# Attention in quads of heads: the last keys of four heads as one unit of 64x64 quadrants, totals in two passes, wider exponentials, three weight blocks without ScalarE

## The chip, the cores and the metric

The kernel runs on one core of one Trainium2 chip. The metric is the time of one execution on the device, in microseconds (us). TensorE is called PE here, VectorE DVE, ScalarE ACT, GpSimd POOL and SyncE SP, as in the profile; PEld is PE's load of weights. Nearly all bulk transfers are issued by SP.

## The reference

Soft-capped attention over 24 heads (2 batches of 12) of 448 tokens and 64 features, followed by two feed-forward layers of 768 to 2048 to 768 features on the 896 tokens:

```python
scores = scale * np.matmul(q, k.transpose(0, 1, 3, 2))
scores = cap * np.tanh(scores / cap)
attn = np.exp(scores - np.max(scores, axis=-1, keepdims=True))
attn = attn / (np.sum(attn, axis=-1, keepdims=True) + 1e-09)
attn_out = np.matmul(attn, v)
...
h = x @ w_in          # x: attention's result, 896 x 768
g = np.where(h >= 1, h, np.where(h <= -1, 0.0, (h + 1) ** 2 / 4))
x = g @ w_out
...
h = x @ moe2_w_in
out = np.maximum(0.01 * h, h) @ moe2_w_out
```

The attention is in float32. The weights of the layers arrive as 64-bit numbers; the kernel turns each into a float32 and splits that, like the activations, into a rounded high part and a low rest, so that a product of the layers is three matmuls (high by high, low by high, high by low).

## The kernel before

**Attention.** The heads are taken in pairs `i` (12 of them). The 448 keys of a head are three full chunks of 128 and a last one of 64. `scores(i, c)` multiplies the keys of chunk `c` by all 448 queries: the two heads of the pair lie in the two halves of the 128 rows of PE's array, so that a unit is two matmuls of 64 rows by 128 columns. The last chunk is different: POOL copies the 64 last keys of both heads into a block-diagonal tile `KL` (and the values into `VL`, L310), and the unit is four matmuls of 128 rows by 32 columns, half of whose stationary operand is zero. ACT takes the tanh of a unit out of PSUM (L336, 896 elements per partition, 448 for the last chunk) and the exponential over two chunks at once in SBUF (L339, 1792 and 1344 elements). `values(i, c)` multiplies the exponentials by the values, in four matmuls of 128 by 32 per chunk, and adds up over the chunks in one of two PSUM tiles that alternate from pair to pair. `sums` adds the exponentials of the three full chunks on DVE (L354); `totals`, in `normalize`, sums them over the keys by a matmul with ones (L364), four matmuls of 128 by 32. The rest of `normalize` brings the result to SBUF (L380), collects the totals by four small transfers (L372), takes the reciprocal (L376), spreads it over the partitions by way of DRAM (L385, L387) and leaves the result as a high and a low part, `xh` and `xl` (L389 to L392).

**Order.** Nothing is ordered by hand on the five engines. Each step is a task of `Plan` with a cost and what it reads and writes; PE's tasks keep the order in which the program adds them, and `Plan.order` places all others by when they could start and by how urgent they are. The order is then fixed: each engine, and SP's queue, works it off from first to last.

**Layers.** `weights(g)` loads block `g` (768 KB for the first layer) and makes the high and low part: an absolute value on ACT (L223), a clamp, a shift and two combinations on DVE (L204 to L217), the high part by a copy on ACT (L228), the low part on DVE. The first four blocks are loaded and made while attention still runs. Then 2304 matmuls of 128 by 128 by 448 columns follow, of the lines 237, 238 and 241. The first 18 of them (`in_part(0, ...)`, batch 0) stand within the last pair, so that PE has work while the last exponentials are taken; then come the other three blocks for batch 0, then the first four feature chunks of batch 1, and last the two that hang on the results of the last heads.

Of the kernel before, what the change touches and what calls it, by code (L numbers as in the profile page):

```python
# [19 lines left out]
LOW_30 = 0x3FFFFFFF  # L20

# [103 lines left out]
def tile_softcap_attention_ffn_ffn(  # L125
# [67 lines left out]
    def weights(g, after=()):  # L193
# [29 lines left out]
        add("ACT", act(n) + 0.06, lambda: nc.scalar.activation(f32(w), f32(r[:, :, 1]), AF.Abs), R, [W])  # L223
# [4 lines left out]
        add("ACT", act(n), lambda: nc.scalar.copy(h, f32(w)), [W], [H])  # L228
# [18 lines left out]
    NIN, NE, NX = 3, 2, 4  # L247
    WARM = 7

    Q = [ap.tile([P, S], F32, name=f"q{n}") for n in range(NIN)]  # L250
    K = [ap.tile([P, S], F32, name=f"k{n}") for n in range(NIN)]
    KL = [ap.tile([P, P], F32, name=f"kl{n}") for n in range(NIN)]

    V = [ap.tile([P, NC, P], F32, name=f"v{n}") for n in range(NIN)]
    VL = [ap.tile([P, P], F32, name=f"vl{n}") for n in range(NIN)]
# [3 lines left out]
    E = [[ap.tile([P, k, S], F32, name=f"e{x}{n}") for n, k in enumerate((4, 3))] for x in range(NE)]  # L259
    T = [ap.tile([P, 2, S], F32, name=f"t{n}") for n in range(NE)]  # L260
    XS = [ap.tile([P, 2, S], F32, name=f"xs{n}") for n in range(NX)]
    zero = ap.tile([P, S], F32, name="zero")
    CS = [ap.tile([P, 2, SP7], F32, name=f"cs{n}") for n in range(NX)]
    RC = [ap.tile([P, SP7], F32, name=f"rc{n}") for n in range(NX)]
    BC = [ap.tile([P, S], F32, name=f"bc{n}") for n in range(NX)]
    XF = [ap.tile([P, S], F32, name=f"xf{n}") for n in range(NX)]
    RR = [dram.tile([2, S], F32, name=f"rr{n}") for n in range(NX)]
# [5 lines left out]
    def q_load(i, j, by):  # L273
        by.dma_start(out=Q[i % NIN][HEADS[j]], in_=qt[i][HEADS[j], j])

    def begin():
        nc.scalar.dma_start(out=K[0], in_=kt[0])
        for j in range(2):
            q_load(0, j, nc.scalar if j else nc.sync)
# [3 lines left out]
        for _ in range(WARM):  # L283
            nc.tensor.matmul(DS[3][:, 0, :S], z[:, :P], z, start=True, stop=True)
# [4 lines left out]
        for n in range(NIN):  # L289
            nc.gpsimd.memset(KL[n], 0.0)  # L290
            nc.gpsimd.memset(VL[n], 0.0)
# [7 lines left out]
    def loads(i):  # L299
        z = i % NIN  # L300
        if i:
            dma(lambda: nc.sync.dma_start(out=K[z], in_=kt[i]), P * S * 4, (), [("k", z)])
            for j in range(2):
                dma(lambda j=j: q_load(i, j, nc.sync), D * S * 4, (), [("q", z, j)])
        dma(lambda: nc.sync.dma_start(
            out=V[z].rearrange("p c x -> p (c x)"), in_=vt[i].rearrange("p c j d -> p (c j d)")), P * NC * P * 4, (), [("v", z)])

        def last(to, src, at):
            for r, x in zip(HEADS, at):
                nc.gpsimd.tensor_copy(to[r, r], src[r, x:x + LAST])  # L310

        add("POOL", 0.6, lambda: last(KL[z], K[z], (S - LAST, 0)), [("k", z)], [("kl", z)])
        add("POOL", 0.6, lambda: last(VL[z], V[z][:, L], (0, D)), [("v", z)], [("vl", z)])

    def part(i, c):

        return E[i % NE][c // 2][:, c % 2 * 2:c % 2 * 2 + (1 if c == L else 2)]

    def scores(i, c):
        z, t = i % NIN, i * NC + c  # L320
        d, e = DS[t % 2], part(i, c)
        last = c == L
        whole, key = E[i % NE][c // 2], ("e", i % NE, c // 2)

        def mm():
            if last:
                for r in COLS4:
                    nc.tensor.matmul(d[r, 0, :S], KL[z][:, r], Q[z], start=True, stop=True)  # L328
                return
            for j, r in enumerate(HEADS):  # L330
                at = c * P + (LAST if j else 0)
                nc.tensor.matmul(d[:, j, :S], K[z][r, at:at + P], Q[z][r], start=True, stop=True)  # L332

        n = 1 if last else 2
        add("PE", PE_F, mm, [("kl" if last else "k", z), ("q", z, 0), ("q", z, 1)], [("d", t % 2)])
        add("ACT", act(n * S, 1), lambda: nc.scalar.activation(e, d[:, :n, :S], AF.Tanh, scale=rcap),  # L336
            [("d", t % 2)], [key])
        if c % 2:
            add("ACT", act((2 + n) * S, 1), lambda: nc.scalar.activation(whole, whole, AF.Exp, scale=capb), [], [key])  # L339

    def values(i, c):
        z, e, a = i % NIN, part(i, c), DS[2 + i % 2]
        v = VL[z] if c == L else V[z][:, c]

        def mm():
            for n, r in enumerate(COLS4):
                nc.tensor.matmul(a[r, 0, :S], v[:, r], e[:, 0 if c == L else n // 2], start=(c == 0), stop=(c == L))  # L347

        add("PE", PE_F, mm, [("e", i % NE, c // 2), ("vl" if c == L else "v", z)], [("d", 2 + i % 2)])

    def sums(i, c):

        t = T[i % NE]
        add("DVE", vec(2 * S), lambda: nc.vector.tensor_tensor(  # L354
            out=t, in0=part(i, 0) if c == 1 else t, in1=part(i, c), op=ALU.add), [("e", i % NE, c // 2)], [("t", i % NE)])

    def normalize(i):
        a, t, e = DS[2 + i % 2], T[i % NE], part(i, L)

        def totals():  # L360

            for n, r in enumerate(COLS4):
                w, x = (ones[0], t[:, n]) if n < 2 else (ones[n - 1], e[:, 0])
                nc.tensor.matmul(a[r, 1, :S], w, x, start=True, stop=True)  # L364

        add("PE", PE_F, totals, [("e", i % NE, 1), ("t", i % NE)], [("d", 2 + i % 2)])
        y = i % NX
        xs, cs, rc, bc, xf, rr = XS[y], CS[y], RC[y], BC[y], XF[y], RR[y]

        def total(k, j):  # L370
            row = k * D + j * Q4
            nc.sync.dma_start(out=cs[HEADS[j], k], in_=xs[row:row + 1, 1])  # L372

        def recip():
            nc.vector.tensor_tensor(out=cs[:, 0], in0=cs[:, 0], in1=cs[:, 1], op=ALU.add)
            nc.vector.reciprocal(out=rc, in_=cs[:, 0])  # L376

        b, hp = divmod(i, NP)
        hi, lo = (x[:, hp, b * S:(b + 1) * S] for x in (xh, xl))
        add("DVE", vec(2 * S), lambda: nc.vector.tensor_copy(xs, a[:, :, :S]), [("d", 2 + i % 2)], [("xs", y)])  # L380
        for k in range(2):
            for j in range(2):
                dma(lambda k=k, j=j: total(k, j), 0, [("xs", y)], [("cs", y, k, j)], more=1.0)
# [9 lines left out]


    later = {}
    turn = [0]

    def bank():
        turn[0] += 1
        return (2, 0, 1, 3)[(turn[0] - 1) % 4]  # L400
# [75 lines left out]
    for i in range(NIN - 1):  # L476
        loads(i)
# [112 lines left out]
```

## Time and profile before

| what | before |
|---|---|
| median of 3 runs | 567.0 us (565.86 to 567.14) |
| the profiled execution's own time | 566.49 us |
| its span (first to last instruction) | 564.7 us |
| PE busy | 558.3 us (99%) |
| DVE busy | 396.8 us (70%) |
| ACT busy | 273.3 us (48%) |
| POOL busy | 21.4 us (4%) |
| bytes read from HBM, written | 61.74 MB, 2.80 MB |

The span is 1.8 us shorter than the execution's time. Busy shares are means over a program with two very different stages: attention until about 100 us after the start, the layers from there on. PE is busy nearly always in both, so its busy share alone can't tell how much of its time is needed; for that, the starts of its instructions have to be read, one group after the other. The records of a float32 matmul come in twos (it runs as two passes), so a unit of two matmuls shows as x4 and a unit of four as x8.

### The profile page before, as it was taken

Reading aid. Unit: us, or ns where it says so; the run is one execution under the profiler, and the core shown is the slowest. Engines: PE = TensorE matmul, PEld = TensorE weight load, DVE = VectorE, ACT = ScalarE, POOL = GpSimd, SP = SyncE. Lnnn points to the kernel's source line nnn. Section 1 sums busy time; section 2 is a strip of 40 time slices with the busy share of each in tenths; the row PEclk is TensorE's granted clock in tenths of the full one; section 3 lists DMA queues with packets and bytes.
Section 4 is the critical chain, followed back from the end, with each engine's and each line's share of the span. In section 5 each row is a group of like instructions: output and inputs, shape, how many; then the busy total and the mean of one; then the engine's idle time right before and its main releaser. Section 6 shows DMA issues by size and latency. Waiting matters only on the chain.

```text
span 564.7 us, 7882 instructions
## 1 busy us (share of the span) xinstructions
PE 558.3 (99%) x3031; PEld 463.7 (82%) x3031; DVE 396.8 (70%) x586; ACT 273.3 (48%) x332; POOL 21.4 (4%) x64
## 2 busy tenths in 40 slices
PE   8999999999999999999999999999999999999997
PEld 4332334899999999999999999999999999999996
DVE  2486979849999987756665859988877755646420
ACT  6999998047666655332332335544444432232210
POOL 4221210000000000000000000000000000000000
PEclk9999999999999999999999999999999999999999
DMA  8454653423333323443324333433323144453400
GB/s 223 142 156 139 163 142 94 142 73 112 113 113 115 106 79 95 129 113 111 110 81 156 140 111 114 156 122 113 96 79 107 38 125 132 139 142 93 136 33 34
DMA packets 27622, 65.14 MB, mean 115 GB/s; under 512 B 8384, under 2 KB 14528, under 8 KB 27584
## 3 DMA queue, kind: packets, MB, share of 16 engines
q1 hardware_dynamic: 27328, 64.29, 37.6%
q8 instruction: 24, 0.39, 0.3%
q10 hardware_dynamic: 224, 0.34, 0.2%
q14 instruction: 14, 0.11, 0.1%
q0 software_dynamic: 32, 0.00, 0.0%
HBM read 61.74 MB, written 2.80 MB: 114 GB/s over the span
## 4 chain that ended last, share of the span: by engine, by line
PE 95%; ACT 1%; DMA 1%; DVE 1%; issue 0%; SPq 0%; DVEq 0%; ACTq 0%; POOLq 0%
PE d L237 27%; PE d L241 27%; PE d L238 27%; PE d L347 6%; PE d L332 4%; PE d L364 2%; PE d L328 1%; DMA capb<-cap 1%; ACT e L336 1%; ACT e L339 1%; DMA cs<-xs 0%; DVE t L354 0%; SPq L372 0%; DVE w L212 0%; DVE w L208 0%
## 5 line engine op out<-in xcount | busy, mean ns | idle before, releaser
L237 PE MATMUL d<-gh,whi 128*128 128x448 f32 x384 | 140.3, 365 | 0.0
L238 PE MATMUL d<-gl,whi 128*128 128x448 f32 x384 | 140.2, 365 | 0.0
L237 PE MATMUL d<-xh,whi 128*128 128x448 f32 x384 | 139.5, 363 | 0.0
L238 PE MATMUL d<-xl,whi 128*128 128x448 f32 x384 | 139.2, 362 | 0.0
L228 ACT CAST whi<-w 128x512 fp32r<-128x512 f32 (+1 forms) x80 | 56.4, 705 | 137.7 <-PE d L238 89.3
L241 PE MATMUL d<-xh,wlo 128*128 128x448 f32 x384 | 111.9, 362 | 0.0
L241 PE MATMUL d<-gh,wlo 128*128 128x448 f32 x384 | 111.7, 365 | 0.0
L171 DVE TENSOR_TENSOR wlo<-w,whi 128x512 fp32r<-128x512 f32 (+1 forms) x80 | 63.4, 792 | 54.3 <-ACT whi L228 54.2
L237 PEld LDWEIGHTS d<-xh,whi 128*128 128x128 f32 x384 | 72.1, 188 | 6.5 <-DVE xs L380 0.7
L241 PEld LDWEIGHTS d<-gh,wlo 128*128 128x128 f32 x384 | 72.1, 188 | 5.7
L237 PEld LDWEIGHTS d<-gh,whi 128*128 128x128 f32 x384 | 72.1, 188 | 5.7
L238 PEld LDWEIGHTS d<-gl,whi 128*128 128x128 f32 x384 | 72.1, 188 | 5.7
L241 PEld LDWEIGHTS d<-xh,wlo 128*128 128x128 f32 x384 | 72.1, 188 | 4.7
L238 PEld LDWEIGHTS d<-xl,whi 128*128 128x128 f32 x384 | 72.1, 188 | 4.7
L223 ACT ACTIVATE w<-wr 128x512 f32<-128x512 f32 (+1 forms) x80 | 61.4, 767 | 16.2 <-DVE wlo L171 6.7
L212 DVE SCALAR_TENSOR_TENSOR w<-wr,w 128x512 int32<-128x512 int32 (+1 forms) x80 | 63.9, 798 | 2.4
L216 DVE SCALAR_TENSOR_TENSOR w<-wr,w 128x512 int32<-128x512 int32 (+1 forms) x80 | 63.8, 797 | 2.4
L429 DVE TENSOR_TENSOR a<-d,a 128x896 f32<-128x896 f32 x32 | 34.7, 1086 | 16.2 <-ACT a L428 15.8
L336 ACT ACTIVATE e<-d,rcap 128x896 f32<-128x896 f32 (+1 forms) x48 | 41.4, 909 | 7.2 <-PE d L332 3.9
L208 DVE TENSOR_SCALAR w<-w 128x512 int32<-128x512 int32 (+1 forms) x80 | 38.5, 481 | 2.7
L204 DVE TENSOR_SCALAR w<-w 128x512 f32<-128x512 f32 (+1 forms) x80 | 37.7, 472 | 3.5 <-ACT w L223 3.5
L339 ACT ACTIVATE e<-e,capb 128x1792 f32<-128x1792 f32 (+1 forms) x24 | 38.5, 1603 | 0.8
(48 smaller groups left out, 373.8 us busy)
## 6 DMA issues: line engine op xcount, KB each, us to landing
wr<-w1o SPq DMA_DIRECT2D x24, 512.0 KB, 3.6
wr<-w2i SPq DMA_DIRECT2D x16, 768.0 KB, 4.3
wr<-w2o SPq DMA_DIRECT2D x24, 512.0 KB, 3.7
wr<-w1i SPq DMA_DIRECT2D x11, 768.0 KB, 4.3
wr<-w1i SPq DMA_DIRECT2D x15, 256.0 KB, 3.2
v<-vt SPq DMA_DIRECT2D x12, 256.0 KB, 3.3
bc<-rr SPq DMA_DIRECT2D x24, 112.0 KB, 4.0
out<-a SPq DMA_DIRECT2D x12, 224.0 KB, 4.3
```

What stands on the lines that cost most here:

```text
L171: nc.vector.tensor_tensor(out=out_, in0=x, in1=f32(hi), op=ALU.subtract)
L204: nc.vector.tensor_scalar(out=f32(w), in0=f32(w), scalar1=W_MIN, scalar2=W_MAX, op0=ALU.max, op1=ALU.min)
L208: nc.vector.tensor_scalar(out=w, in0=w, scalar1=3, scalar2=LOW_30, op0=ALU.logical_shift_left, op1=ALU.bitwise_and)
L212: nc.vector.scalar_tensor_tensor(out=w, in0=r[:, :, 1], scalar=SIGN_AND_TOP, in1=w, op0=ALU.bitwise_and, op1=ALU.bitwise_or)
L216: nc.vector.scalar_tensor_tensor(out=w, in0=r[:, :, 0], scalar=29, in1=w, op0=ALU.logical_shift_right, op1=ALU.bitwise_or)
L223: add("ACT", act(n) + 0.06, lambda: nc.scalar.activation(f32(w), f32(r[:, :, 1]), AF.Abs), R, [W])
L228: add("ACT", act(n), lambda: nc.scalar.copy(h, f32(w)), [W], [H])
L237: nc.tensor.matmul(o[:, b, :S], ch, h[:, f, r], start=first, stop=False)
L238: nc.tensor.matmul(o[:, b, :S], ch, l[:, f, r], start=False, stop=False)
L241: nc.tensor.matmul(o[:, b, :S], cl, h[:, f, r], start=False, stop=last)
L336: add("ACT", act(n * S, 1), lambda: nc.scalar.activation(e, d[:, :n, :S], AF.Tanh, scale=rcap), [("d", t % 2)], [key])
L339: add("ACT", act((2 + n) * S, 1), lambda: nc.scalar.activation(whole, whole, AF.Exp, scale=capb), [], [key])
```

## The change

Attention is now done in steps `j` of two pairs, that is four heads (6 steps).

- The last keys of the four heads are one unit, `AB`: each head's 64 keys by 64 features take one quadrant of 64 by 64 of PE's array, four matmuls, without the zeros, so the tiles `KL` and `VL` and POOL's copies go. A step has seven units (A0, A1, A2 of the first pair, B0, B1, B2 of the second, and AB) for scores and seven for values, where two pairs had eight and eight.
- The results of a step are added up in one PSUM tile (bank 0 for the first pair, bank 1 for the second); the other three tiles are a ring for scores and totals. Before it was two and two.
- The totals of a step are one unit of its own in a slot of the ring, in two passes: first AB's exponentials against ones, then the sums of the full chunks.
- The exponentials are taken over groups of two, three and two units (1792, 2688 and 1792 elements). They have one, two and one buffers.
- Queries, keys and values are loaded for two pairs at a time, in two buffers instead of three of one pair; the reciprocals and the last steps of `normalize` run over two pairs at once.
- For the first three weight blocks the absolute value and the copy are done by DVE (`early`).
- At the end, the 18 matmuls of `in_part(0, ...)` stand in three pieces of 6 around the last values and totals, and the last two feature chunks of batch 1 are one piece.

```diff
-    def weights(g, after=()):
+    def weights(g, after=(), early=False):
...
+        def absolute():
+            nc.vector.tensor_scalar(out=w, in0=r[:, :, 1], scalar1=LOW_31, scalar2=None, op0=ALU.bitwise_and)
...
+        if early:
+            add("DVE", vec2(n), absolute, R, [W])
+        else:
+            add("ACT", act(n) + 0.06, lambda: nc.scalar.activation(f32(w), f32(r[:, :, 1]), AF.Abs), R, [W])
...
+        if early:
+            add("DVE", vec2(n), lambda: nc.vector.tensor_copy(h, f32(w)), [W], [H])
...
+    A0, A1, A2, B0, AB, B1, B2 = UNITS = range(7)
+    GROUPS = [(A0, A1), (A2, B0, AB), (B1, B2)]
+    CHUNK = {A0: (0, 0), A1: (0, 1), A2: (0, 2), B0: (1, 0), B1: (1, 1), B2: (1, 2)}
+    WHERE = {u: (g, n) for g, us in enumerate(GROUPS) for n, u in enumerate(us)}
+    NE = [1, 2, 1]
...
+    RING, AV = 3, 3
+    def slot():
+        ring[0] += 1
+        return (ring[0] - 1) % RING
...
+    def scores(j, u):
+        z, s = j % NIN, slot()
...
+            for h, r in enumerate(HEADS):
+                if u == AB:
+                    at = 0 if h else S - LAST
+                    for p, c in enumerate(HEADS):
+                        nc.tensor.matmul(d[c, h, :S], K[z][r, p, at:at + LAST], Q[z][r, p], start=True, stop=True)
+                    continue
+                p, c = CHUNK[u]
+                at = c * P + (LAST if h else 0)
+                nc.tensor.matmul(d[:, h, :S], K[z][r, p, at:at + P], Q[z][r, p], start=True, stop=True)
...
+    def values(j, u):
...
+                if u == AB:
+                    for p, k in enumerate(HEADS):
+                        nc.tensor.matmul(DS[AV][r, p, :S], V[z][k, p, L, r], e[k, h], start=False, stop=p == 0)
+                    continue
...
+    def results(j):
+        y = j % NX
+        for p in range(2):
+            add("DVE", vec(S), lambda p=p: nc.vector.tensor_copy(XS[y][:, p], DS[AV][:, p, :S]), [("av", p)], [("xs", y, p)])
...
+            for x in range(2):
+                for n, r in enumerate(COLS4):
+                    p, h = divmod(n, 2)
+                    w, e = (ones[0], T[j % NT2][p][:, h]) if x else (ones[1 + p], part(j, AB)[:, h])
+                    nc.tensor.matmul(DS[s][r, 0, :S], w, e, start=x == 0, stop=x == 1)
...
+    for j in range(NQ + 1):
+        now, prev = j < NQ, j > 0
+        if now:
+            units(scores, j, (A0, A1))
...
+        else:
...
+            in_part(0, first[0], [0], range(2))
+        if prev:
+            units(values, j - 1, (B1, B2))
+            results(j - 1)
+        if now:
+            units(scores, j, (A2, B0, AB))
+            sums(j, 1)
+        else:
+            in_part(0, first[0], [0], range(2, 4))
...
+        if prev:
+            normalize(j - 1)
+            if j + 1 < NQ:
+                loads(j + 1)
+        if now:
+            units(values, j, (A0, A1))
+            units(scores, j, (B1, B2))
+            sums(j, 2)
...
+            units(values, j, (A2, B0, AB))
```

The first place is PE's queue in the middle of attention. Before, one pair (`d_66`, `d_67` are the tiles for scores, `d_68`, `d_69` those for results and totals; L332 and L328 are scores, L347 values, L364 totals):

```order
L332 MATMUL d_66<-q_88,k_91 128x448 x2
L328 MATMUL d_67<-q_88,kl_94 32x448 x4
L347 MATMUL d_68<-e_105,v_97 32x448 x8
L332 MATMUL d_66<-q_89,k_92 128x448 x2
L332 MATMUL d_67<-q_89,k_92 128x448 x2
L347 MATMUL d_68<-e_106,v_97 32x448 x4
L347 MATMUL d_68<-e_106,vl_100 32x448 x4
L364 MATMUL d_68<-t_109,ones_102 32x448 x2
L364 MATMUL d_68<-e_106,ones_103 32x448
L364 MATMUL d_68<-e_106,ones_104 32x448
```

Now, from A2 to the end of a step; ahead of these rows the step has A0 and A1 and the values of the last step's B1 and B2 (L360 and L356 are scores, L381 and L377 values, L412 totals; `d_69` holds the results):

```order
L360 MATMUL d_68<-q_87,k_89 128x448 x2
L360 MATMUL d_66<-q_87,k_89 128x448 x2
L356 MATMUL d_67<-q_87,k_89 64x448 x4
L412 MATMUL d_68<-e_98,ones_94 32x448 x2
L412 MATMUL d_68<-e_98,ones_95 32x448 x2
L412 MATMUL d_68<-t_102,ones_93 32x448 x2
L412 MATMUL d_68<-t_103,ones_93 32x448 x2
L381 MATMUL d_69<-e_96,v_91 32x448 x8
L360 MATMUL d_66<-q_87,k_89 128x448 x2
L360 MATMUL d_67<-q_87,k_89 128x448 x2
L381 MATMUL d_69<-e_97,v_91 32x448 x8
L377 MATMUL d_69<-e_97,v_91 64x448 x4
```

The shape of the last keys' unit and its place changed, and the totals of the step before now stand in the middle of a step, in the slot that A2 of this step has just left.

The second place is ACT's queue in the middle of attention. Before, with the absolute value (L223) and the copy (L228) of the second weight block between tanh (L336) and exponentials (L339):

```order
L336 ACTIVATE e_105<-d_66,rcap 128x896
L336 ACTIVATE e_105<-d_67,rcap 128x896
L339 ACTIVATE e_105<-e_105,capb 128x1792
L223 ACTIVATE w_73<-wr_71 128x768
L336 ACTIVATE e_106<-d_66,rcap 128x896
L336 ACTIVATE e_106<-d_67,rcap 128x448
L339 ACTIVATE e_106<-e_106,capb 128x1344
L336 ACTIVATE e_107<-d_66,rcap 128x896
L336 ACTIVATE e_107<-d_67,rcap 128x896
L339 ACTIVATE e_107<-e_107,capb 128x1792
L228 CAST whi_76<-w_73 128x768
```

Now, one whole step (L365 is tanh, L368 the exponential):

```order
L365 ACTIVATE e_96<-d_67,rcap 128x896
L365 ACTIVATE e_96<-d_68,rcap 128x896
L368 ACTIVATE e_96<-e_96,capb 128x1792
L365 ACTIVATE e_97<-d_66,rcap 128x896
L365 ACTIVATE e_97<-d_67,rcap 128x896
L365 ACTIVATE e_97<-d_68,rcap 128x896
L368 ACTIVATE e_97<-e_97,capb 128x2688
L365 ACTIVATE e_99<-d_67,rcap 128x896
L365 ACTIVATE e_99<-d_68,rcap 128x896
L368 ACTIVATE e_99<-e_99,capb 128x1792
```

In the new queue no weight block stands between the first tanh and the last exponential of attention: blocks 0 to 2 are DVE's, and block 3 comes after the last exponential.

The third place is DVE's queue at the end of attention: how the results of the last heads (`xf_131` before, `xf_116` now) come out. Before:

```order
L204 TENSOR_SCALAR w_73<-w_73 128x768
L208 TENSOR_SCALAR w_73<-w_73 128x768
L212 SCALAR_TENSOR_TENSOR w_73<-wr_71,w_73 128x768
L389 TENSOR_TENSOR xf_130<-xs_113,bc_126 128x448
L391 CAST xh<-xf_130 128x448
L171 TENSOR_TENSOR xl<-xf_130,xh 128x448
L216 SCALAR_TENSOR_TENSOR w_73<-wr_71,w_73 128x768
L389 TENSOR_TENSOR xf_131<-xs_114,bc_127 128x448
L391 CAST xh<-xf_131 128x448
L171 TENSOR_TENSOR xl<-xf_131,xh 128x448
```

Now:

```order
L216 SCALAR_TENSOR_TENSOR w_72<-wr_70,w_72 128x768
L220 SCALAR_TENSOR_TENSOR w_72<-wr_70,w_72 128x768
L431 TENSOR_TENSOR xf_115<-xs_104,bc_113 128x896
L433 CAST xh<-xf_115 128x2x448
L172 TENSOR_TENSOR xl<-xf_115,xh 128x2x448
L208 TENSOR_SCALAR w_73<-w_73 128x768
L212 TENSOR_SCALAR w_73<-w_73 128x768
L216 SCALAR_TENSOR_TENSOR w_73<-wr_71,w_73 128x768
L220 SCALAR_TENSOR_TENSOR w_73<-wr_71,w_73 128x768
L431 TENSOR_TENSOR xf_116<-xs_105,bc_114 128x896
L433 CAST xh<-xf_116 128x2x448
L172 TENSOR_TENSOR xl<-xf_116,xh 128x2x448
```

The last results now come for two pairs at once, and two weight blocks (`w_72` is block 4, `w_73` block 5) stand ahead of them.

## Rows read from the trace of the kernel before

**Rows 1.** The page, busy time of each engine and its share of the span:

```profile
PE 558.3 (99%) x3031; PEld 463.7 (82%) x3031; DVE 396.8 (70%) x586; ACT 273.3 (48%) x332; POOL 21.4 (4%) x64
```

**Rows 2.** A window in mid-attention: length, busy by engine, granted clock, DMA share, GB/s:

```profile
30.00:40.00 10.00, 10.00 (x88) 3.02 (x84) 8.25 (x12) 9.55 (x10) 2.15 (x4) 1.00 0.53 156
```

**Rows 3.** Waits of PE after its first pair: in total, times, longest:

```profile
PE d L364 <- DVE t L354: 0.2, 1, 0.2
```

**Rows 4.** Timeline, PE over one pair: start, length, operation, count, idle time ahead:

```profile
60.95 1.02 PE L332 MATMUL d<-q,k 64*128 64x448 f32 x4
61.91 0.96 PE L328 MATMUL d<-q,kl 128*32 128x448 f32 x8
62.68 1.69 PE L347 MATMUL d<-e,v 128*32 128x448 f32 x16
64.30 1.77 PE L332 MATMUL d<-q,k 64*128 64x448 f32 x8
66.00 0.96 PE L347 MATMUL d<-e,v 128*32 128x448 f32 x8
66.78 0.94 PE L347 MATMUL d<-e,vl 128*32 128x448 f32 x8
67.53 0.55 PE L364 MATMUL d<-t,ones 128*32 128x448 f32 x2
68.40 1.02 PE L332 MATMUL d<-q,k 64*128 64x448 f32 x4
```

**Rows 5.** Timeline, ACT in the same pair:

```profile
65.39 1.90 ACT L336 ACTIVATE e<-d,rcap 128x896 f32<-128x896 f32 x2 [0.35 <-PE d L332]
67.33 1.79 ACT L339 ACTIVATE e<-e,capb 128x1792 f32<-128x1792 f32 x1
```

**Rows 6.** ACT by line and shape, 0 to 130 us: count, busy, mean ns:

```profile
L336 ACT ACTIVATE e<-d,rcap 128x896 f32<-128x896 f32 x36 | 34.9, 1003 | 7.2 <-PE d L332 3.9 <-DVE rcap L297 3.2
L339 ACT ACTIVATE e<-e,capb 128x1792 f32<-128x1792 f32 x12 | 21.5, 1790 | 0.4
L339 ACT ACTIVATE e<-e,capb 128x1344 f32<-128x1344 f32 x12 | 17.0, 1416 | 0.4
```

**Rows 7.** DVE by line and shape, 0 to 130 us:

```profile
L354 DVE TENSOR_TENSOR t<-e 128x896 f32<-128x896 f32 x12 | 13.0, 1082 | 3.9 <-ACT e L339 3.9
L389 DVE TENSOR_TENSOR xf<-xs,bc 128x448 f32<-128x448 f32 x12 | 7.5, 629 | 7.5 <-DMA bc<-rr 7.5
L212 DVE SCALAR_TENSOR_TENSOR w<-wr,w 128x768 int32<-128x768 int32 x7 | 6.7, 959 | 0.2
L208 DVE TENSOR_SCALAR w<-w 128x768 int32<-128x768 int32 x7 | 3.9, 564 | 0.2
```

**Rows 8.** Timeline, the first pairs, PE and ACT:

```profile
1.39 2.98 PE L284 MATMUL d<-zero 128*128 128x448 f32 x7 [1.39 <-DVE half L286]
...
6.41 1.90 ACT L336 ACTIVATE e<-d,rcap 128x896 f32<-128x896 f32 x2 [3.17 <-DVE rcap L297]
...
8.34 1.79 ACT L339 ACTIVATE e<-e,capb 128x1792 f32<-128x1792 f32 x1
...
10.18 1.71 PE L347 MATMUL d<-e,v 128*32 128x448 f32 x16 [0.77 <-ACT e L339]
...
19.27 1.77 PE L332 MATMUL d<-q,k 64*128 64x448 f32 x8
```

**Rows 9.** Timeline, the end of attention, PE and DVE:

```profile
100.26 0.47 PE L237 MATMUL d<-xh,whi 128*128 128x448 f32 x1
...
100.78 0.36 PE L241 MATMUL d<-xh,wlo 128*128 128x448 f32 x1
...
102.18 0.36 PE L237 MATMUL d<-xh,whi 128*128 128x448 f32 x1
...
116.67 0.62 DVE L389 TENSOR_TENSOR xf<-xs,bc 128x448 f32<-128x448 f32 x1 [3.92 <-DMA bc<-rr]
...
117.75 0.63 DVE L171 TENSOR_TENSOR xl<-xf,xh 128x448 fp32r<-128x448 f32 x1
```

More of the change, by code (lines that the diff above doesn't have):

```diff
@@ L246, in tile_softcap_attention_ffn_ffn @@
     dram = st.enter_context(tc.tile_pool(name="dram", bufs=1, space=bass.MemoryType.DRAM))
-    NIN, NE, NX = 3, 2, 4
+    NIN, NT2, NX = 2, 2, 2
     WARM = 7
[L250 to L255, printed above, removed]
-    ones = [ap.tile([P, Q4], F32, name=f"ones{n}") for n in range(3)]
@@ L297, in begin @@
         nc.vector.tensor_scalar_mul(rcap, rcap, 1.0 / float(D) ** 0.5)
[L299 to L323, printed above, removed]
-        def mm():
[L326 to L339, printed above, removed]
@@ L341, in values @@
-    def values(i, c):
-        z, e, a = i % NIN, part(i, c), DS[2 + i % 2]
-        v = VL[z] if c == L else V[z][:, c]
-        def mm():
[L346 to L355, printed above, removed]
@@ new lines, in sums @@
+    def sums(j, g):
+        k = [key(j, n) for n in range(3)]
+        x = {u: part(j, u) for u in CHUNK}
+        ta, tb = T[j % NT2]
+        for on, p, t, a, b in ((0, 0, ta, x[A0], x[A1]), (1, 0, ta, ta, x[A2]), (2, 1, tb, x[B0], x[B1]), (2, 1, tb, tb, x[B2])):
+            if g == on:
+                add("DVE", vec(2 * S), lambda t=t, a=a, b=b: nc.vector.tensor_tensor(out=t, in0=a, in1=b, op=ALU.add),
+                    k[1:] if on == 2 and a is not tb else [k[g]], [("t", j % NT2, p)])
@@ L474, in pieces, with due @@
         return begun[BEGUN_AT[g]:BEGUN_AT[g] + PIECES]
[L476 to L478 removed]
+    def due():
         for g in range(BEGUN):
[L480 to L501 removed]
@@ L502, in tile_softcap_attention_ffn_ffn, with units @@
-    for f in range(1, BEGUN):
+            if len(begun) == BEGUN_AT[g] + PIECES:
+                weights(g, pieces(g), early=g < BEGUN - 1)
+    def units(f, j, us):
+        for u in us:
+            f(j, u)
+    for j in range(NIN):
+        loads(j)
+    for j in range(NQ + 1):
+        now, prev = j < NQ, j > 0
+        if now:
+            units(scores, j, (A0, A1))
+            sums(j, 0)
+            begun.append(plan.last_pe)
+            due()
+        else:
+            order4.extend([slot(), slot(), slot(), AV])
+            first = [bank() for _ in range(BEGUN)]
+            in_part(0, first[0], [0], range(2))
[5 more added lines that the diff above has]
+            sums(j, 1)
+        else:
+            in_part(0, first[0], [0], range(2, 4))
+            ring[0] += 2
+        if prev:
[6 more added lines that the diff above has]
+            sums(j, 2)
+            begun.append(plan.last_pe)
+            due()
+            units(values, j, (A2, B0, AB))
```

161 lines of the change are left out of this document (89 added, 72 removed).

## The prediction

> **What bounds the kernel now.** I read four views, from coarse to fine. The page says that PE is busy 99% of the span [rows 1], and the window in mid-attention shows all of 10 us on PE at a granted clock of 1.00, the 2.4 GHz level, but also 9.55 us on ACT [rows 2]: either could be the bound. The waits decide it. After its first pair PE waited once in attention, 0.2 us for a sum [rows 3], while ACT, ahead of its tanh, waited 0.35 us for PE's scores [rows 5]. So PE sets the pace and ACT follows closely. What a pair costs is read from the starts on PE [rows 4]: from 60.95 to 68.40, that is 7.45 us, and the starts of its groups are 0.96, 0.77, 1.62, 1.70, 0.78, 0.75 and 0.87 apart. A unit takes 0.75 us whichever way the array is cut: two matmuls of 64x128 (x4, half of the 1.62 to 1.70 us steps less a switch) and four of 128x32 (x8, 66.78 to 67.53) alike. A pair has nine: three scores and one for the last keys, three values and one, one for totals. 9 x 0.75 is 6.75; the rest is four changes between 64x128 and 128x32, at 0.21 (60.95 to 61.91), 0.12 (62.68 to 64.30), 0.20 and 0.12, and 0.05 of small change. Four heads cost 14.9 us.
>
> **The change, part by part.** *PE.* The program's order gives a step of four heads seven units of scores, seven of values and two of totals: 16 x 0.75 = 12.0 us, where two pairs had 18. What goes is one unit of scores and one of values, the half of the last keys' work that multiplied zeros. A step has eight changes of shape, as two pairs had. Four are of the known kinds, 0.20 + 0.12 + 0.12 + 0.20 = 0.64 us. Four lead to or from the quadrants, which this trace does not show. The known changes cost 0.12 to 0.21; I take the mean, 0.16, four times 0.64 us. Below, a change could be free (two shapes of 64 rows); above, I allow 0.35, the longest pause that the rows show between two engines' instructions [rows 5]. A step is then 12.0 + 1.28 = 13.3 us, between 12.6 and 14.0, and 1.6 us less than before.
>
> The quadrants' unit itself is not shown either. I price it at 0.75 us, since the rows show two and four tiles of the array working at once at that same price [rows 4], and four quadrants are the product of the two cuts. Its other end, one quadrant after the other, is 4 x 0.75 = 3.0 us, a rival below. The Trainium skill (TensorE: Matmul & The Clock Gate, Part 3, Measured speedup vs the span model) lists packings that fall short: four row tiles gave 3.07 times, not four. By that the unit would cost about 0.98 us and the sum 2.7 us more, by estimate; here the trace speaks against it, for four column tiles cost no more than two row tiles.
>
> *ACT.* A step has seven tanh, two exponentials of 1792 and one of 2688. By the mean durations [rows 6] that is 7 x 1.00 + 2 x 1.79 + 2.54 = 13.1 us (the 2.54 is 1.79 plus twice the 0.375 between the two lengths shown). Back to back two tanh take 1.90, not 2.01 [rows 5], which makes it 12.5. No weight block stands there any more. So ACT needs 12.5 to 13.1 in a step of 13.3 on PE: still second, with less room than the rows suggest at first.
>
> *Where PE can wait for ACT.* Scores start their tanh 1.09 us after the unit begins (64.30 to 65.39 [rows 4, 5]). Counting from a step's start: A0 and A1 through tanh by 3.0, their exponential by 4.8, A2's tanh by 5.75. PE in the meantime does A0, A1 (1.5), the old B1, B2 (to 3.2), A2, B0, AB (to 5.75 with their changes) and wants the totals at 5.9, in A2's slot. That is 0.15 us of room, the tightest place. The values of A2, B0, AB are wanted at 10.7 and their exponential is done at 10.2; the last exponential of the step ends at 13.9 and is wanted 1.7 us into the next step, at 15.0.
>
> *DVE.* Sums: four of 1.08 as before [rows 7]. The copies out of PSUM are three of 448 elements at about 0.63, where there were two of 896 at the price of a sum. The normalization runs once over 896. That makes about 9.2 us per step. An early block adds two operations: the copy at 0.56 by L208's row, the absolute value between 0.56 and the 0.96 of L212, which reads the same strided half; with the other five a block is 5 to 5.5 us. A step with a whole block holds 14.7 us of DVE work in 13.3 us, a lag of 1.4. It costs nothing as long as the sums of a step, due about 2.7 us into the next, come before the totals at 5.9: 3 us of cover. Without that cover each us of lag is a us of PE.
>
> *One tile for results.* A0's values at 7.4 need only bank 0, complete when the old AB ends before the step begins; B0's at 11.5 need bank 1, complete at 3.2. Each copy is 0.63 us: hidden by over 4 us.
>
> *Transfers.* SP's queue has 11 entries per step where two pairs had 22, half of them twice as large. Keys and queries of step j+1 may be issued when the scores of j-1 are done, about 13 us before they are wanted; even a wait like the 3.9 us for a transfer [rows 9] would fit three times. In the stretch shown the DMA engines were busy 0.53 of the time [rows 2]. POOL's copies were off the path, and saving them is worth nothing.
>
> *Start.* ACT waits until 6.41 for the cap [rows 8], and this stays. From there three tanh end at 9.3, the first exponential at 11.0, two more tanh at 12.9, the wide exponential at 15.4; PE then does three units of values (2.4) and begins step 1 at 18.0. Before, the third pair began at 19.27 [rows 8]. Gain 1.3 us, paid with longer pauses of PE, about 1.8 us ahead of the first values and 1.2 us ahead of the wide group's.
>
> *End.* Step 5 begins at 18.0 + 4 x 13.3 = 71.2. It takes 13.15 without its last change, then 6 matmuls of the layer (0.20 apart [rows 9], 1.35 with the change), values B1, B2 (1.6), 6 more (1.35), totals (1.6): PE is through with attention at 90.25, with 12 of the layer's matmuls done. Before it was at 100.26 [rows 9], with 18 done. Gain 10.0 less 6 x 0.20 = 8.8 us.
>
> *A new wait.* The last results before were complete at 117.75 + 0.63 = 118.4, 18.1 us after the totals, with a wait of 3.9 for a transfer [rows 9]; PE wanted them 19.8 us after (99 matmuls at 0.20). Now they come for two pairs: twice the length in the last three operations (+1.2), twice the bytes in the spread, less the 0.5 saved in the copy ahead, so 18.8 to 20.5; PE wants them after 96 matmuls, 19.2. I charge 0.5 us, between 0 and 1.5.
>
> **Sum.** Span 564.7 - 8.8 + 0.5 = 556.4; with the 1.8 us outside the span the profiled execution would be 558.2. It was 0.5 us below the median before, so I forecast a median of 558.7 us, a gain of 8.3. The four unknown changes move it by -3.5 to +4.2 over five and a half steps.
>
> **The rivals.**
> - *Two quadrants at a time*, so that the last keys are not one unit. Nothing in the rows shows rows and columns of the array cut together. AB costs 1.5 us, twelve times 0.75 more: 567.7, no change. This is the change not doing what it says. Chance 0.08.
> - *One quadrant at a time.* Then 12 x 2.25 = 27 us more: 585.7, slower. It decides as soon as an AB unit takes over 1.44 us (8.3 / 12 more than 0.75). Against it: the rows' four tiles at 0.75. Chance 0.06.
> - *PE waits for ACT or DVE in every step*, at the totals (0.15 us of room) or behind a lagging sum. If A2's tanh comes 0.7 us late, as it would were ACT's step 13.1 and its own waits not hidden, five steps cost 3.5 us: 562.2. For it: 9.55 of 10 us on ACT; against it: PE hardly ever waited [rows 3] although ACT then carried the weights too. Chance 0.13.
> - *The clock falls in the first step.* Before, PE paused 0.77 us and the next 16 records took 1.71 us [rows 8], as in mid-attention (1.69 [rows 4]), so no slower. The new pause is 1.8 us. The seven first matmuls took 0.43 us each [rows 8] against 0.20 in the layers; were four units at that pace, it would add 3 us: 561.7. The Trainium skill (TensorE: Matmul & The Clock Gate, Part 1) says that the clock falls back to 1.2 GHz after PE has been idle long enough; no row here shows it. Chance 0.05.
> - *The quadrants' changes are free* or PE gains elsewhere: about 555. Chance 0.04.
>
> **How the numbers follow.** The forecast has 0.64. Its own bounds and the two rivals around 562 lie between 555 and 563, which leaves out the two rivals of the quadrants and little else. 0.3% of 567.0 is 1.7 us, about what a measurement of this kernel can tell from no change. Faster by more: 0.64 + 0.13 + 0.05 + 0.04, less 0.01 for their upper tails, 0.85. Slower by more: one at a time 0.06, and 0.03 of two at a time with waits on top, 0.09. Within it: the rest, 0.06.
>
> **What would show it.** Starts on PE in a step: AB's eight records 0.75 us, the step 13.3, changes to and from quadrants 0.1 to 0.2. PE's waits: none at the totals beyond a few tenths. ACT: idle about 0.2 to 0.8 us per step, and no weight instruction before the last exponential. Step 1 at 18, totals of step 5 done near 90, a wait of PE for `xl` below 1.5 us. Wrong would be an AB unit near 1.5 or 3.0 us, a step above 14, a granted clock under 1.00 after the first pauses, or DVE's sums ending after the totals are due.

## The result: 559.3 us, and the profile after

The changed kernel took 559.34 us in the median of four runs (558.62 to 561.50), the kernel before 566.75 us on the same chip: ratio 0.9874, 95% interval 0.9849 to 0.9899. The forecast was 558.7. The profiled run took 558.62 us, its span 556.8 us. In some lists of runs single executions lie 10 us or more above the rest: the ratios leave those out, the medians do not, and the one profile taken in such an execution is that of experiment 5.

The page of the changed kernel: the busy times, and the chain of work that ended last (as shares of the span):

```profile
PE 549.4 (99%) x2935; PEld 461.4 (83%) x2935; DVE 394.4 (71%) x562; ACT 265.0 (48%) x314; POOL 1.4 (0%) x10
...
PE 97%; ACT 2%; issue 0%; DVE 0%
```

PE's busy time fell by 8.9 us [rows 1] and the span by 7.9. Here is one step of four heads on PE, and then that step as one window (columns as in [rows 2]):

```profile
45.20 1.77 PE L360 MATMUL d<-q,k 64*128 64x448 f32 x8
46.90 1.71 PE L381 MATMUL d<-e,v 128*32 128x448 f32 x16
48.54 1.77 PE L360 MATMUL d<-q,k 64*128 64x448 f32 x8
50.25 0.98 PE L356 MATMUL d<-q,k 64*64 64x448 f32 x8
51.16 0.96 PE L412 MATMUL d<-e,ones 128*32 128x448 f32 x8
51.93 0.94 PE L412 MATMUL d<-t,ones 128*32 128x448 f32 x8
52.69 1.69 PE L381 MATMUL d<-e,v 128*32 128x448 f32 x16
54.30 1.77 PE L360 MATMUL d<-q,k 64*128 64x448 f32 x8
56.01 1.71 PE L381 MATMUL d<-e,v 128*32 128x448 f32 x16
57.65 0.98 PE L377 MATMUL d<-e,v 64*64 64x448 f32 x8
58.56 1.77 PE L360 MATMUL d<-q,k 64*128 64x448 f32 x8
```

```profile
45.20:58.56 13.36, 13.36 (x108) 4.25 (x105) 8.78 (x11) 12.62 (x11) 0.00 (x0) 1.00 0.61 180
```

The step is 13.36 us, where two pairs took 14.90 [rows 4]. The quadrants' eight records start 0.91 us before the totals (50.25 to 51.16): one unit of 0.75 and a change of shape. PE is busy all the time, ACT 12.62 us, and the only wait that ACT's rows show in the step stands ahead of A0's tanh:

```profile
46.29 1.91 ACT L365 ACTIVATE e<-d,rcap 128x896 f32<-128x896 f32 x2 [0.56 <-PE d L360]
48.23 1.79 ACT L368 ACTIVATE e<-e,capb 128x1792 f32<-128x1792 f32 x1
49.93 2.79 ACT L365 ACTIVATE e<-d,rcap 128x896 f32<-128x896 f32 x3
52.75 2.54 ACT L368 ACTIVATE e<-e,capb 128x2688 f32<-128x2688 f32 x1
```

The next rows show the start and the end of attention, in the form of [rows 8, 9]: ACT's first tanh, PE where the layers resume after the totals, DVE's last results, and PE where it wants them.

```profile
7.02 2.80 ACT L365 ACTIVATE e<-d,rcap 128x896 f32<-128x896 f32 x3 [3.79 <-PE d L360]
...
91.38 0.47 PE L247 MATMUL d<-xh,whi 128*128 128x448 f32 x1
...
107.79 1.09 DVE L431 TENSOR_TENSOR xf<-xs,bc 128x896 f32<-128x896 f32 x1 [1.34 <-DMA bc<-rr]
108.92 0.63 DVE L433 CAST xh<-xf 128x896 fp32r<-128x896 f32 x1
109.58 1.09 DVE L172 TENSOR_TENSOR xl<-xf,xh 128x896 fp32r<-128x896 f32 x1
...
110.69 0.36 PE L247 MATMUL d<-xh,whi 128*128 128x448 f32 x1
110.89 0.36 PE L248 MATMUL d<-xl,whi 128*128 128x448 f32 x1
```

The first tanh now waits for PE's scores, not for the cap (ready at 5.88). The layers resume at 91.38, 8.88 us earlier than at 100.26 [rows 9], with 12 of their matmuls done instead of 18 (6 x 0.20 = 1.2 us): 7.7 of the span's 7.9 us. The last `xl` is done at 110.67 and wanted at 110.89: no wait, with 0.2 us to spare.

### The profile page after: what moved, and what is told of

Same layout as the page of the kernel before. It is cut to its first block, busy times and chain, and to the rows that moved or that the text cites. A ratio compares the mean times of both kernels' runs of the same rounds, so it can differ in the third digit from the quotient of the medians.

```text
span 556.8 us, 7429 instructions
## 1 busy us (share of the span) xinstructions
PE 549.4 (99%) x2935; PEld 461.4 (83%) x2935; DVE 394.4 (71%) x562; ACT 265.0 (48%) x314; POOL 1.4 (0%) x10
## 4 chain that ended last, share of the span: by engine, by line
PE 97%; ACT 2%; issue 0%; DVE 0%
PE d L247 28%; PE d L251 28%; PE d L248 28%; PE d L360 5%; PE d L381 5%; PE d L412 2%; PE d L377 1%; PE d L356 1%; ACT e L365 1%; ACT e L368 1%; PE d L312 1%; ACT a L505 0%; DVE zero L309 0%; DVE half L314 0%
## 5 line engine op out<-in xcount | busy, mean ns | idle before, releaser
L238 ACT CAST whi<-w 128x512 fp32r<-128x512 f32 (+1 forms) x77 | 54.0, 701 | 146.2 <-PE d L248 96.7
L230 ACT ACTIVATE w<-wr 128x512 f32<-128x512 f32 (+1 forms) x77 | 58.5, 760 | 18.7 <-DMA wr<-w1i 8.8
L365 ACT ACTIVATE e<-d,rcap 128x896 f32<-128x896 f32 x42 | 39.6, 1002 | 6.5 <-PE d L360 6.0
L368 ACT ACTIVATE e<-e,capb 128x1792 f32<-128x1792 f32 (+1 forms) x18 | 36.7, 2038 | 0.5
```

The costliest lines, as they stand in the source:

```text
L365: add("ACT", act(2 * S, 1), lambda: nc.scalar.activation(e, d[:, :, :S], AF.Tanh, scale=rcap), [("d", s)], [key(j, g)])
```

## The experiments

All edits but the seventh are to the changed kernel. Ratios are to the kernel before, run beside them on the same chip. "Step 1" is the start of PE's second step, "`xl` done" the end of the last `xl` counted from where the layers resume, both from the profiled run and in us (the changed kernel's first profile: 18.47 and 19.3).

| kernel | median us | ratio, 95% interval | step 1 | `xl` done |
|---|---|---|---|---|
| 1 unchanged | 559.54 | 0.9858 (0.9834 to 0.9882) | 20.06 | 19.5 |
| 2 reciprocal earlier | 558.86 | 0.9849 (0.9827 to 0.9871) | 19.86 | 19.6 |
| 3 weights on ACT again | 560.32 | 0.9856 (0.9826 to 0.9885) | 18.34 | 19.3 |
| 4 two more quadrant units | 565.94 | 0.9974 (0.9959 to 0.9989) | 17.47 | 19.5 |
| 5 one exponential cut | 564.80 | 0.9946 (0.9924 to 0.9969) | 17.00 | 23.0 |
| 6 all exponentials cut | 558.42 | 0.9845 (0.9816 to 0.9874) | 17.23 | 19.9 |
| 7 before, weights on DVE | 567.60 | 1.0003 (0.9984 to 1.0023) | | |
| 8 ten first matmuls | 559.77 | 0.9849 (0.9812 to 0.9886) | 18.55 | 21.0 |
| 9 cut in step 0 alone | 558.93 | 0.9847 (0.9826 to 0.9868) | 17.22 | 19.7 |
| 10 spread ahead of the load | 557.77 | 0.9830 (0.9808 to 0.9851) | 17.48 | 18.6 |
| 11 9, 10 and 2 together | 558.90 | 0.9847 (0.9824 to 0.9871) | 16.40 | 19.4 |
| 12 5 and 10 together | 557.80 | 0.9832 (0.9806 to 0.9859) | 19.26 | 18.0 |

### Where the gain comes from

**Experiment 4, two more units of quadrants in each step.** It repeats the scores of the last keys, which leaves the results as they are.

```diff
-            for h, r in enumerate(HEADS):
+            for h, r in [*enumerate(HEADS)] * (3 if u == AB else 1):
```

> The scores of the quadrants' unit are computed three times instead of once (the same values into the same place): two more units per step on PE, as many as the change took out, nothing else. Theory: PE sets the pace and a quadrants' unit costs 0.75 us, so each step grows by 1.5 us and the kernel by 6 x 1.5 = 9.0, less what the first step hides (up to 1.0): 566.6 to 567.8, about the time of the kernel before. Rival (ACT's relief is the gain, PE had slack): well under 9, say 2 to 5 us, since PE's extra work would lie under ACT's.

```profile
52.26 2.49 PE L356 MATMUL d<-q,k 64*64 64x448 f32 x24
54.67 0.96 PE L412 MATMUL d<-e,ones 128*32 128x448 f32 x8
```

The three units take 2.41 us to the next group's start instead of 0.91, and the step 14.87 (17.47 to 32.34) instead of 13.36: 0.755 us per unit. Each us of work put on PE lengthens the step by a us, so PE sets the pace and the two units that the change took away are its gain. The median rose by 6.4 us over experiment 1's, where five such steps make 7.5. The first step hides its two units: step 1 began at 17.47 with them, and at 17.48 without them in experiment 10, whose first tanh came at nearly the same time (6.04, here 6.02). Between these two profiles the spans differ by 7.6 us (563.5 and 555.9), as five steps do; why the medians differ by a us less is not shown.

**Experiment 3, the weights of blocks 0 to 2 back on ACT**, and **experiment 7, the same move alone in the kernel before** (its diff is the part of the change on `weights` and `early`).

```diff
-                weights(g, pieces(g), early=g < BEGUN - 1)
+                weights(g, pieces(g), early=False)
```

> The three early weight blocks' absolute value and copy go back to ACT; all else as in the change. Theory: PE sets the pace with only 0.2 to 0.8 us of room on ACT per step, so one weight instruction of 0.83 to 0.93 us in a step pushes tanh past PE's need at the totals: the four steps with one grow by 0.3 to 0.5 us each, in all 1 to 2 us more than the change, about 560 to 561. Rival A (the change's gain is the relief of ACT, PE's units do not matter): it gives back most of the 7.4 us, 564 or more. Rival B (ACT has room to spare): no difference, within 0.4 us.

> The kernel before with one part of the change alone: blocks 0 to 2 have their absolute value and copy done by DVE. Theory (PE set the pace before as well; ACT's weight work was hidden): pairs stay 7.45 us, time 567.0 within 1 us. Rival (ACT at 9.55 of 10 us was holding PE in places, and the change owes a part of its gain to this move): 564 to 566. Third: DVE's longer blocks delay sums and PE waits at the totals: 568 or more.

```profile
45.51 0.82 ACT L238 CAST whi<-w 128x768 fp32r<-128x768 f32 x1
46.23 1.90 ACT L365 ACTIVATE e<-d,rcap 128x896 f32<-128x896 f32 x2
```

In experiment 3 the copy lies in ACT's pause ahead of A0's tanh and the steps stay 13.36 (45.06 to 58.42 on PE). My theory fell: a step has room for an instruction of 0.8 to 0.9 us. In experiment 7 the pairs stay 7.44 us (18.75 to 26.19) and the time does not move, although DVE's longer blocks made PE wait once for a sum, 0.87 us at 93.54. The part on the weights is worth nothing that can be measured, in either kernel.

**Experiments 5, 6 and 12, narrower exponentials.** 5 cuts the middle one as shown; 6 has `[[0, 1, 2], [0, 1, 2, 3], [0, 1, 2]]`; 12 is below.

```diff
+    CUTS = [[0, 2], [0, 2, 3], [0, 2]]
...
+            for a, b in zip(CUTS[g], CUTS[g][1:]):
+                some = whole[:, a:b]
...
+                    lambda some=some: nc.scalar.activation(some, some, AF.Exp, scale=capb), [], [key(j, g)])
```

> The changed kernel, but the exponential over 2688 elements is cut in two, 1792 and 896, as pairs had it: undoes the wider exponentials alone. The three lengths seen (1344: 1.42 us, 1792: 1.79, 2688: 2.54) give a fixed part of about 0.29 us, so ACT's load grows by 0.29 us in a step of 13.36, of which it idles 0.55. Theory (PE sets the pace, ACT has 0.55 us of room): step stays 13.36, ACT's idle time ahead of A0's tanh falls to about 0.26, time 559.3, no change against the changed kernel. Rival (ACT's order inside the step is tight: the totals wait for A2's tanh, the values for the wide exponential, so that a delay of 0.29 us shows on PE although ACT idles elsewhere): the step grows by up to 0.29 to 13.65, time up to 560.9.

> The changed kernel with an exponential for each unit (seven of 896 elements in a step). Each takes about 1.04 us by the same line, so ACT's load grows by 7 x 1.04 - 6.11 = 1.17 us, past its idle 0.55. Theory (ACT's room is what it idles): ACT becomes the bound, steps of 13.36 + 0.62 = 14.0 us, ACT idle near nothing, PE waits about 0.6 per step, time 559.3 + 5 x 0.62 = about 562.5. Rival (room elsewhere: ACT's tanh overlap their reads and it keeps pace): steps 13.4, time 559.5. Second rival (tight order): steps 14.5, time about 565.

In 5 the steps are 13.37 (44.35 to 57.72 on PE) and ACT's pause is still 0.56. Only step 1 is longer, 13.99, which pays back an early start as in experiment 9. The cut costs nothing in attention, and its 5 us were lost at the tail (below). In 6 too the undisturbed step is 13.37 (31.08 to 44.45): one exponential of 896 alone takes 1.04 us, but three in a row 2.90, so ACT's load rose by less than I had worked out. Step 1 took 13.85, ACT being still behind from the start; step 3 took 13.70, and step 5 lost 1.45 us, because PE waited for DVE there:

```profile
52.82 2.90 ACT L372 ACTIVATE e<-e,capb 128x896 f32<-128x896 f32 x3
```

```profile
74.73 1.71 PE L385 MATMUL d<-e,v 128*32 128x448 f32 x16 [1.45 <-DVE rc L424]
```

In the order these values have a wait for DVE that they lack in the changed kernel, whose DVE copies the results of both pairs together, later; here the first copy (73.96 to 74.58) stands right ahead of the reciprocal that the row names. So neither theory held as stated: the wide exponentials are worth nothing here, and what a cut does cost comes from how it shifts the order of other engines.

### The start

**Experiment 1, the changed kernel again.**

> The changed kernel once more, to learn its scatter: its four runs reached from 558.6 to 561.5 us, those of the kernel before only from 565.9 to 567.1. My theory: attention is bound by PE and takes the same time in every run (13.36 us per step); the scatter comes from its end, where the last results arrive 0.1 us before PE wants them, so that any late transfer makes PE wait. It expects steps of 13.3 to 13.4 us in this profile too, and, if the profiled run is a long one, the excess as a wait of PE for xh or xl near 110 us. Rival: the scatter comes from the first step (transfers at the start), then step 1 begins later than 18.5 us in a long run.

The late end, my theory, fell: `xl` came 19.5 us after the layers resumed, as in the first profile, but step 1 began 1.59 us later and the span was 1.8 longer. The rival, the first step, held. Loads of weights on PE and ACT's first tanh in this run:

```profile
5.60 0.68 PEld L360 LDWEIGHTS d<-q,k 64*128 64x128 f32 x4 [0.80 <-DMA q<-qt]
...
9.50 0.33 PEld L360 LDWEIGHTS d<-q,k 64*128 64x128 f32 x1 [0.23 <-issue]
10.20 0.19 PEld L360 LDWEIGHTS d<-q,k 64*128 64x128 f32 x1 [0.37 <-issue]
```

```profile
7.50 1.01 ACT L365 ACTIVATE e<-d,rcap 128x896 f32<-128x896 f32 x1 [4.26 <-PE d L360]
8.99 1.01 ACT L365 ACTIVATE e<-d,rcap 128x896 f32<-128x896 f32 x1 [0.49 <-PE d L360]
```

A load takes 0.33 us until 9.5 and 0.19 from 10.2: PE runs at half pace until then, and two tanh lie 1.49 us apart. This is the granted clock, though the views print 1.00 all through: the trace's own record of it begins only at 10.15 us, at the 2.4 GHz level, and a stretch without a record is printed as 1.00. The record begins at 6.69 in the changed kernel's first profile and at 4.23 in experiment 4 (first tanh at 6.02). In each of these runs it lies between the last load of 0.33 us and the first of 0.19, and in experiment 5, where the record shows the 1.2 GHz level later on (below), the loads take 0.33 us again.

The clock is one of two causes. PE also waited for a transfer of queries, 0.80 us here, 0.48 in the first profile, not at all in experiment 10 (first tanh at 6.04), and longest in experiment 12, whose first tanh came at 8.28:

```profile
6.38 0.51 PEld L361 LDWEIGHTS d<-q,k 64*128 64x128 f32 x4 [1.58 <-DMA q<-qt]
```

**Experiment 8, ten instead of seven first matmuls** (`WARM = 10`).

> The changed kernel with 10 instead of 7 first matmuls on zeros (0.43 us each). Four runs of the kernel began step 1 at 17.5 to 20.1 us, according to when PE's pace doubled (4.3 to 10.2 us after the start). Theory (PE's pace doubles after it has been kept at work long enough; the later units pause for ACT and lose it): scores begin 1.3 us later, at 5.6, but all at full pace; first tanh at 6.7 to 7.0, step 1 at 18.0 to 18.5 in every run, profiled time near 558.5 and less scatter between runs (median 558.5). Rival (the moment is set by something else, at random, whatever PE does): first tanh 7.3 to 9, step 1 at 18.5 to 21, median 560 to 561, same scatter.

The scores began at 5.42 and their four units took 3.89 us, nearly all at full pace (6.81 in experiment 1). That fits the theory but doesn't show it: the clock's record begins at 5.98, inside the range of the runs with seven, and with seven the four units took 3.95 us in experiment 10. The first tanh came at 7.09, no earlier than at 7.02, and step 1 at 18.55, so the longer wait gives back what the pace gains. The three runs of its ratio scatter no less (558.5 to 560.4).

**Experiment 9, the cut of the exponentials in step 0 alone**, `CUTS = [[0, 1, 2], [0, 1, 2, 3], [0, 2]]` for `j == 0`.

> The changed kernel, but in step 0 alone the exponentials of the first two groups are taken unit by unit (896 elements each), so that values need not wait for a whole group. In the changed kernel PE waits there 1.40 and 0.95 us. With seven exponentials of 896 in every step these waits were 0.65 us and none, step 1 began at 17.23, but PE then waited 1.7 us for DVE in later steps, whose order had moved. Theory (the start is on the path, the rest untouched): step 1 begins 1.5 to 1.8 us earlier than at the same pace of PE, near 16.8, steps stay 13.36, time 557.5 to 558.0 against 559.4. Rival (what is won at the start is lost at the tail, where the last results come when they come): time 559.0 to 559.5, with PE waits for xh or xl of over 1 us.

Step 1 began at 17.22, but step 2 at 31.93, where the changed kernel had 31.83. PE's waits of 1.40 and 0.95 became 0.51, then 0.93 and 0.27 a step later:

```profile
19.93 1.71 PE L385 MATMUL d<-e,v 128*32 128x448 f32 x16 [0.93 <-ACT e L372]
```

Both theories fell. From its first tanh to step 2 ACT is never idle in the changed kernel, and step 2 begins 24.8 us after it at full pace of PE (7.02 to 31.83; 7.09 to 31.91 in experiment 8; 6.04 to 30.85 in 10). So the start is ACT's: the groups decide only where PE waits, and the moment of the first tanh decides the rest, as long as PE is at full pace from there on (25.9 us in experiment 1, where ACT waited twice more for scores).

### The tail

**Experiment 2, the last reciprocal earlier in DVE's order.**

```diff
-                0, [("sm", y)], [("cs", y, n)], more=1.0)
+                0, [("sm", y)], [("cs", y, n)], more=-1.0 if j == NQ - 1 else 1.0)
```

> Only the order on DVE at the end is changed: the last reciprocal stands ahead of a weight block's low part, clamp and shift instead of behind them. Theory of the end: the last results come about 1.4 us earlier (reciprocal at 96.6 instead of 98.0), the fastest runs stay at 558.6 us, the slow ones vanish: median 558.6 to 559.0, all runs within 0.6 us. Rival (the scatter comes from the start or elsewhere): the median stays near 559.3 and the runs still spread over 2 us or more.

The reciprocal came 4.7 us after the layers resumed instead of 6.7, `xl` no earlier: the spread was issued at 104.53, 6.5 us behind the 98.00 of the small transfer that it waits for (4.7 us in experiment 1). That one now stood 0.57 us behind the start of a weight load in SP's queue (97.43). No gain.

What a late tail costs was seen in **experiment 5**. These are PE's waits in its profile, and windows (columns as in [rows 2]):

```profile
PE d L247 <- DVE xh L437: 2.4, 1, 2.4
PE d L248 <- DVE xl L172: 0.4, 1, 0.4
```

```profile
112.00:116.00 4.00, 3.14 (x7) 2.43 (x8) 1.51 (x2) 0.08 (x1) 0.00 (x0) 0.56 0.00 0
116.00:120.00 4.00, 4.00 (x14) 3.57 (x13) 2.22 (x4) 3.54 (x5) 0.00 (x0) 0.59 0.00 0
120.00:125.00 5.00, 5.00 (x26) 4.53 (x25) 4.93 (x6) 5.00 (x7) 0.00 (x0) 1.00 0.00 0
```

The spread `bc`, issued at 102.99, 0.42 us behind a weight load, was awaited until 110.66. PE waited 2.4 us for `xh` and 0.4 for `xl`. At the end of the first wait its granted clock fell: the trace records the 1.2 GHz level from 112.49 to 119.32, of which the windows show the means 0.56 and 0.59, and the matmuls stood 0.37 us apart instead of 0.20. That is 2.8 us of waits and about 3 of pace (14 matmuls 0.17 us too far apart, and two of 0.74 us ahead of them), about the 5 us of this kernel's median. Eleven of its twelve runs show a mean clock of 0.994 to 0.997; the twelfth, with 0.999, took 560.32 us. That those other runs waited at the same place is inferred from their clock, as only one has a trace. In experiment 8 the spread took 7.5 us (102.02 to 109.56), PE waited 0.43 and 0.65 us, and the clock stayed at 1.00.

**Experiments 10 to 12: the spread goes ahead of the load.**

```diff
-        weights(f, pieces(f) if f < len(BEGUN_AT) else ())
+        weights(f, pieces(f) if f < len(BEGUN_AT) else (), behind=spread[-2:] if f in (6,) else ())
```

(`behind` makes the load of block 6 depend on the last two spreads.) 11 adds the edits of 9 and 2, 12 the cut of 5.

> The changed kernel, but the load of weight block 6 (768 KB) goes onto SP's queue behind the last spread of the reciprocals (bc) instead of just ahead of it. In four traces with the load ahead, the spread took 5.0 to 7.7 us from its issue to the product that waits for it, and where it took over 7 PE waited for xh and xl: 1.1 us in the run with 10 first matmuls, 2.8 us in the one with the cut exponential, where PE's granted clock then fell to 0.56 for 7 us. Theory (the load takes the spread's bandwidth): the spread takes 3 to 4 us, xl is done 1 to 3 us earlier counted from the totals (17 to 18.5 us after them instead of 19.5), PE waits for nothing there, time 558.6 with less scatter (no run above 560.5). Rival (the spread's time is its own, its many small pieces): 5 us as before, time 559.3, same scatter. Second rival: the load comes too late and PE waits for block 6, over 560.

> Both edits together, and the last reciprocal moved ahead of the low part of block 3 on DVE. If start and tail each give what the theories say and do not hang on each other: step 1 near 16.8, xl done 16 to 18 us after the totals, no wait of PE there, time 557.0 (556.5 to 557.8), faster than the changed kernel by 2.0 to 2.5. If the tail eats the start's gain (the rival of the first edit): 558.5 to 559.5.

> The cut of the 2688 exponential into 1792 and 896 again, with the spread ahead of the load as in the second kernel of this call. Its first run had a median of 564.8, with steps of 13.36 as in the changed kernel, and lost its time at the tail (waits for xh and xl of 2.8 us, then half pace). Theory (the cut costs nothing by itself, its shift of DVE's and SP's order made the tail late): steps 13.36, no wait at the tail, clock 1.00 there, time 558.5 to 559.5. Rival (the cut slows the layers in some other way): again 563 to 566.

SP's queue and DVE in experiment 10:

```profile
101.39 1.24 SPq L424 DMA_DIRECT2D bc<-rr  x2
105.42 15.65 SPq L201 DMA_DIRECT2D wr<-w1i  x3
```

```profile
106.10 1.09 DVE L432 TENSOR_TENSOR xf<-xs,bc 128x896 f32<-128x896 f32 x1 [0.75 <-DMA bc<-rr]
```

From issue to product the spread took 4.7 us (10), 5.3 (11) and under 4.8 (12); with the load ahead 5.0 to 7.7. The long cases are gone, but the 3 to 4 us of my expectation did not come. The profiles with the load ahead go by how closely it stands there: issued 2.4 to 2.9 us before the spread, the spread took 5.0 to 5.3 us (the first profile, experiments 1, 2 and 4); 2.1 us before, 6.0 (9); 1.6 to 1.8 us before, 7.1 to 7.5 (6, 8); 0.42 us before, 7.7 (5). A load 2.4 us ahead costs next to nothing, and so there was little to win in most runs. PE waited for nothing at the tail in all three. Experiment 12 settles 5: with the same cut and the spread ahead the median is 557.8, so the 5 us were the tail's. Experiment 11 missed its 557.0: step 1 at 16.40 was paid back by waits of 0.93 and 0.28 in that step, as in 9, and the earlier reciprocal ran its small transfer into a weight load issued at 95.31, as in 2 (the small one was issued at 95.88, the spread only at 101.84).

Experiment 10 has the lowest median, and the runs that its ratio uses lie within 557.63 to 558.23, where eight runs of the changed kernel lay between 558.6 and 561.5. But the intervals of the ratios overlap, and its profiled run owes its 0.9 us to the start (first tanh at 6.04). That it is faster is likely, not shown.

## Why the prediction was right

- **Step of four heads**, 13.3 forecast, 13.36 measured; the quadrants' unit 0.75 forecast, 0.755 measured (experiment 4). The four unknown changes of shape were taken at 0.16; they are 0.21, 0.16, 0.14 and 0.16 (into and out of the quadrants, at 50.25, 51.16, 57.65 and 58.56). Both rivals of the quadrants are out. The Trainium skill (TensorE: Matmul & The Clock Gate, Part 3, Measured speedup vs the span model) gives 3.07 times for four row tiles, by which the unit would be 0.98 us, by estimate; the measurement decides. The bound of 0.35 for a change was called the longest pause that the rows show, though [rows 8] have longer ones; nothing came near it.
- **ACT second with little room.** 12.62 us busy in the forecast's 12.5 to 13.1. (The lower end took the saving of tanh in a row too often: rows of two, three and two make 12.7 by [rows 5, 6].) The totals' 0.15 us of room held, and with it the rival of waits in every step is out. But I read the room too narrowly: a step took in another 0.9 us (experiment 3).
- **Start**: forecast 18.0 for step 1, measured 18.47. The step that failed is "ACT waits until 6.41 for the cap, and this stays": the cap was ready at 5.88, and PE's scores came later, because PE waited 0.48 us for queries and was at half pace until 6.69. In the profile of the kernel before it did not wait for queries and had its full pace from 5.86. (The queries are not late by the change: in experiment 7 PE waited 0.96 us for them.) In other runs the first tanh came at 6.02 to 8.28.
- **End of attention**: 90.25 forecast, 91.38 measured: 0.47 from the start, 0.47 from the steps (five at 13.37 where I had 13.3 and 13.15), 0.19 from the pieces at the end.
- **New wait**: 0.5 us charged; none in the profiled run (span less resumption 465.42 us, and 464.44 + 1.2 before). Start and end together were 1.1 us too early, the tail 0.7 too dear, so the sum of 556.4 came out at 556.8: that it is off by only 0.4 us is luck, as the two misses have opposite signs and no common cause. The mechanism is real, though: 0.2 us of slack here, 1.1 us of wait in experiment 8, and 2.8 with a fallen clock in experiment 5, outside my bound of 1.5.
- **The clock** did not fall in the first step: after PE's pause of 1.40 us the next 16 records took 1.71. It did in experiment 5 after a pause of 2.43. The Trainium skill (TensorE: Matmul & The Clock Gate, Part 1) says that the clock falls back once PE has been idle long enough; experiment 5 shows such a fall.
- **DVE**: no wait of PE for it in the steps; its 3 us of cover held.

Still open are what sets the moment at which PE's clock rises, why the queries come at different times, and which place made the one run of 561.5, of which there is no trace.

## What to carry to other kernels

Where one engine runs without a pause, price a change by that engine's units and its changes of shape, read from starts and not from busy times; here work saved on an engine that follows it closely (weights and wide exponentials on ACT) was worth nothing, even at 95% busy. When attention or any first stage gets shorter, look at the small transfers at its end: here a spread of two times 224 KB queued behind a 768 KB load had 0.2 us of slack. And an edit that looks local can shift the order of other queues, so compare those before reading its time. Last, a clock printed as 1.00 can be a stretch without a record: here the length of the weight loads told the pace.

## What the runs showed of the hardware

- Four tiles of 64 by 64 cost 0.755 us per unit (experiment 4), about the same as two of 64 by 128 or four of 128 by 32 (0.75 in [rows 4]); each change between these shapes costs 0.11 to 0.21 us.
- PE's granted clock came to the 2.4 GHz level anywhere from 4.23 to 10.15 us after the start, in kernels that begin alike; weight loads took 0.33 us before it and 0.19 after. Together with waits of PE for queries, of up to 1.12 us (experiment 2), this moved step 1 from 17.48 (experiment 10) to 20.06 (experiment 1).
- After a pause of 2.43 us the granted clock was at the 1.2 GHz level for 6.8 us and the matmuls ran at about half pace (experiment 5); pauses of 1.40 us (first step) and of 0.43 and 0.65 us (experiment 8) had no such effect.
- Exponentials of 896 in a row stand 0.93 to 0.95 us apart, though one alone takes 1.04 (experiment 6).
- A spread of two times 224 KB took 4.7 to 5.3 us from issue to use with no load or an older one ahead of it in SP's queue, and up to 7.7 us with a 768 KB load issued 0.42 us before it.
